# Linear attention and a Swish layer in one kernel: key-value products moved into the numerators' run, k's exponentials a block ahead of q's

## The chip, the cores and the metric

The kernel runs on one core of a Trainium2 chip. The metric is the device time of one execution in microseconds. Five runs of the kernel before gave a median of 286.03 us (285.89 to 286.53). One more execution was taken by the hardware profiler; all durations below are from that one.

## The reference

Linear attention for 8 batches of 8 heads, 576 positions and 64 channels, then a layer with a scaled Swish on the 4,608 rows of 512 that come out of it. All inputs and the output are float32.

```python
phi = lambda x: np.where(x > 0, x, np.exp(x) - 1.0) + 1.0
q_p, k_p = phi(q), phi(k)
kv  = einsum('bhsd,bhse->bhde', k_p, v);   z = sum(k_p, axis=2)
num = einsum('bhsd,bhde->bhse', q_p, kv)
den = einsum('bhsd,bhd->bhs', q_p, z)[..., None] + 1e-06
x = (num / den) as rows [4608, 512]
h = x @ w_in                              # w_in [512, 2048]
out = (h / (1 + exp(-beta * h))) @ w_out  # w_out [2048, 512]
```

## The kernel before

**Blocks.** One block of the second layer takes 512 rows: the first 512 positions of one batch, in four x tiles. The 64 positions left over of each batch make a ninth block. A block has two stages. In H (`h_phase`, L779) TensorE makes 16 tiles of h, four matmuls of 512 columns each (`h_mm`, L439), and ScalarE turns each into g with Silu (`silu`, L448). In Y (`y_phase`, L790) TensorE makes four tiles of the output, sixteen matmuls each (`y_mm`, L456), VectorE copies each out of PSUM and SyncE's queue writes it out (`y_out`, L469).

**Attention between the lines.** While block b runs, the attention of batch b+1 and b+2 is made in pieces that the program hangs between the matmuls. Two dictionaries, `sh` for H and `sy` for Y, say after which step of the stage a piece is issued (L811 to L834). H has 16 steps, one a tile; Y has 16 too, four a tile. Nothing reorders instructions: each engine works in the order in which they were issued, and tiles bring the waits. For block b, with n = b+1 and m = b+2, the kernel before does this:

- After step 8 of H, `kv_both(n)` (L230): 72 products of 64x64 (`k_quads`, L177) make kv and z of batch n in a PSUM tile of its own, and VectorE copies it to `kvd` (L239). In block 2, `odd_numers` (L335), the left-over numerators of batches 0 and 1, come just before.
- After the last step of H, `numers(n)` (L322): 72 products of 64x64 make the numerators and denominators of batch n, in two PSUM tiles of two banks (`nps`) and in two of the four buffers that H and Y tiles use too (`nps_m`). `norms` (L372) divides them on VectorE into x tiles.
- After steps 0 and 1 of Y, `x_trans_dma(n, t)` (L426): SyncE issues the transposes that bring the x tiles into `xT`, from which the next block's H reads.
- After step 3 of Y, phi of q of batch m (`phi_all`, L487): two exponentials on ScalarE (L144), then on VectorE max and min (L148, L155). phi(x) is min(exp(x), max(x, 0) + 1).
- After step 5 of Y, `q_trans_dma(m)` (L272): SyncE transposes phi of q by DMA. Then GpSimd issues the loads of q and k of batch m+1 (`load_kq`, L476); the q load is held until those transposes have landed (`hold`, L88), and the k load stands behind it in GpSimd's queue.
- After step 8 of Y, phi of k of batch m, and on GpSimd the two copies of v of batch m into `vaug` (`v_copy`, L171).
- After step 9 of Y, SyncE issues the load of v of batch m+1.

**Buffers.** There are three of q and k each (`xq`, `xk`, L51), two of v and `vaug`, four of the exponentials' result (`e`, L143), two of the large PSUM tiles (`num_tile`, L227) and four of the small ones (`mm_tile`, L453).

**Start.** Batch 0, the weights and batch 1 have a stage of their own (L556 to L770); the first block that follows the scheme is b = 1. In it, after step 2 of H, q, k and v of batch 3 are loaded. Two table loads a Y stage (`ACT_TABLE_LOAD`) switch ScalarE between exponential and Silu.

Of the kernel before, what the change touches and what calls it, by code (L numbers as in the profile page):

```python
# [9 lines left out]
BF16 = mybir.dt.bfloat16  # L10
# [6 lines left out]
def kernel(  # L17
# [10 lines left out]
    nc = tc.nc  # L28

    B, H, S, D = q.shape  # L30
    DM = H * D
    DFF = moe_w_in.shape[1]
    P = 128
    KC = DM // P
    FC = DFF // P
# [3 lines left out]
    EA = D + 1  # L39
# [8 lines left out]
    work = ctx.enter_context(tc.tile_pool(name="work", bufs=2))  # L48


    NX = 3  # L51
# [28 lines left out]
    def load(eng, dst, src, b, h0=0, n=4):  # L80

        rows = src[b].rearrange("h (g j) d -> (h g) (j d)", j=J)
        return eng.dma_start(  # L83
            out=dst[:, h0 : h0 + n].rearrange("p h j d -> p h (j d)"),
            in_=rows.rearrange("(i p) e -> p i e", p=P)[:, h0 : h0 + n],
        )

    def hold(d, after):  # L88
        tc.add_manual_dep(d.ins, after.ins.name, SYNC, reason="share of the queues")
# [48 lines left out]
    st = {}  # L138

    def phi_part(b, a, pr, x, j0=0, j1=J):  # L140

        if j0 == 0:
            st[b, a, pr, "e"] = work.tile([P, 2, J, D], BF16, tag="e", name="e", bufs=4)  # L143
        nc.scalar.activation(st[b, a, pr, "e"][:, :, j0:j1], x[:, :, j0:j1], ACTF.Exp)  # L144
# [6 lines left out]
    def phi_tile(b, a):  # L151
        st[b, a] = work.tile([P, 2, J, P], BF16, tag=f"phi{a}", name=f"phi_{a}")

    def phi_min(b, a, pr, j0=0, j1=J):
        nc.vector.tensor_tensor(  # L155
            st[b, a][:, pr, j0:j1].rearrange("p j (h d) -> p j h d", h=2),
            st[b, a, pr, "e"][:, :, j0:j1].rearrange("p h j d -> p j h d"),
            st[b, a, pr, "r"][:, :, j0:j1].rearrange("p h j d -> p j h d"),
            ALU.min,
        )  # L160
# [5 lines left out]
    def xin(b, a, pr):  # L166
        if b == 0 and a == "q":
            return q0f[:, places(b, pr)]
        return (xk if a == "k" else xq)[b % NX][:, places(b, pr)]

    def v_copy(eng, b, pr):  # L171
        src = vb[b % 2] if b == 2 else vf[b % 2]
        eng.tensor_copy(  # L173
            vaug[b % 2][:, pr, :, :, 0:D], src[:, places(b, pr)].rearrange("p h j d -> p j h d")
        )

    def k_quads(b, pr, dst, mov):  # L177

        for j in range(J):
            for h in range(2):  # L180
                for hh in range(2):
                    r = slice(hh * G, (hh + 1) * G)
                    c = slice(h * D, (h + 1) * D)
                    nc.tensor.matmul(  # L184
                        dst[hh][c], st[b, "k"][r, pr, j, c], mov(r, j, h),
                        start=(j == 0), stop=(j == J - 1), skip_group_check=True,
                    )
# [39 lines left out]
    def num_tile(name):  # L227
        return numps.tile([P, 2, 512], F32, tag="num", name=name)

    def kv_both(b):  # L230

        t = num_tile("kvp")
        for pr in range(2):
            k_quads(
                b, pr, [t[:, hh, pr * EA : (pr + 1) * EA] for hh in range(2)],
                lambda r, j, h: vaug[b % 2][r, pr, j, h, 0:EA],
            )
        st[b, "kvd"] = work.tile([P, 2, 2 * EA], BF16, tag="kv_bd", name="kvd")
        nc.vector.tensor_copy(st[b, "kvd"], t[:, :, 0 : 2 * EA])  # L239

# [31 lines left out]
    def q_trans_dma(b):  # L272
        st[b, "qTd"] = work.tile([P, 4 * J, G], BF16, tag="qT", name="qTd")
        for hh in range(2):
            st[b, "qTd", "dma"] = nc.sync.dma_start_transpose(
                out=st[b, "qTd"][:, hh * 2 * J : (hh + 1) * 2 * J],
                in_=st[b, "q"][hh * G : (hh + 1) * G].rearrange("p a j c -> p (a j c)"),
            )
# [40 lines left out]
                e = e0 + 2 * (pr - prs[0]) + hh  # L319
                quads(b, dst, e, lambda c, pr=pr: (pr, 2 * t + c), hh, pr)  # L320

    def numers(b):  # L322
        pairs = [num_tile("nps") for _ in range(2)]
        odd = [mm_tile("nps_m") for _ in range(2)]
        for k in range(2):
            dst = [pairs[k][:, h] for h in range(2)]
            numer_tile(b, dst, k)
            numer_tile(b, dst, 2, (k,), 4)
        numer_tile(b, odd, 3)
        for hh in range(2):  # L330
            quads(b, odd, 4 + hh, lambda c: (c, J - 1), hh, None)
        st[b, "nps"] = pairs, odd


    def odd_numers():  # L335
# [90 lines left out]
    def x_trans_dma(b, t):  # L426
        xv = st[b, "xs", t].rearrange("p n d -> p (n d)")
        if t < NT - 1:
            nc.sync.dma_start_transpose(out=x_dst(b, t), in_=xv)
            return  # L430

        for pr in range(2):
            nc.sync.dma_start_transpose(
                out=xT_tail[:, places(b, pr), b * G : (b + 1) * G],
                in_=xv[pr * G : (pr + 1) * G, 0 : 2 * P],
            )
# [16 lines left out]
    def mm_tile(name):  # L453
        return mmps.tile([P, 512], F32, tag="mm", name=name)

    def y_mm(b, t, i, yp, c0=0, c1=512):  # L456
        for c in range(4):
            ff = 4 * i + c
            nc.tensor.matmul(  # L459
                yp[:, c0:c1],  # L460
                g_sb[b % 2][:, ff, t * P : (t + 1) * P],
                w_out_sb[i][:, c, c0:c1],
                start=(ff == 0), stop=(ff == FC - 1), skip_group_check=True,
            )
# [8 lines left out]
            dst = rows(b, 2 * t + i) if b < B else rows(2 * t + i, J - 1)  # L473
            queues[i].dma_start(out=dst[:, c0:c1], in_=y_sb[i * G : (i + 1) * G, c0:c1])

    def load_kq(b, after=None):  # L476
        if b < B:
            d = load(nc.gpsimd, xq[b % NX], q, b)
            if after is not None:
                hold(d, after)  # L480
            load(nc.gpsimd, xk[b % NX], k, b)

    def load_v(b):
        if b < B:
            load(nc.sync, vf[b % 2], v, b)

    def phi_all(b, a):  # L487
        phi_tile(b, a)
        for pr in range(2):
            phi_part(b, a, pr, xin(b, a, pr))  # L490
        for pr in range(2):
            phi_relu(b, a, pr, xin(b, a, pr))
        for pr in range(2):
            phi_min(b, a, pr)


    beta_c = consts.tile([P, FC], F32)
# [277 lines left out]
    def run(side, n):  # L775
        for f in side.get(n, ()):
            f()

    def h_phase(b, x, side):  # L779
        for ff in range(FC):  # L780

            if b == 1 and ff in (3, 4):
                hp = num_tile("h_ps2")[:, 0]
            else:
                hp = mm_tile("h_ps")
            h_mm(b, x, ff, hp)
            silu(b, ff, hp)
            run(side, ff)

    def y_phase(b, side, last=False):  # L790
        for t in range(4):
            if last and t == 3:
                for c0, c1 in ((0, 320), (320, 512)):
                    yp = mm_tile("y_ps")
                    for i in range(4):
                        y_mm(b, t, i, yp, c0, c1)
                    y_out(b, t, yp, c0, c1, (nc.sync, nc.scalar))
                break
            yp = mm_tile("y_ps")
            for i in range(4):  # L800
                y_mm(b, t, i, yp)
                if i < 3:
                    run(side, 4 * t + i)
            y_out(b, t, yp)
            run(side, 4 * t + 3)

    def at(side, n, *fs):
        side.setdefault(n, []).extend(fs)


    for b in range(1, B + 1):  # L811
        n = b + 1
        sh, sy = {}, {}
        if b == 1:
            at(sh, 0, lambda: q_trans_dma(2))
            at(sh, 1, lambda: [v_copy(nc.gpsimd, 2, pr) for pr in range(2)])
            at(sh, 6, lambda: q_odd_trans(1, num_tile("qop")[:, 0].bitcast(BF16)[:, 0:256]))
            at(sh, 2, lambda: load_kq(3, st[2, "qTd", "dma"]), lambda: load_v(3))
        if b == 2:
            at(sh, 8, odd_numers, odd_norms)  # L820
            at(sh, 9, lambda: [x_trans_dma(i, 4) for i in range(2)])
        if n < B:
            at(sh, 8, lambda: kv_both(n))
            at(sh, FC - 1, lambda: numers(n), lambda: [norms(n, k) for k in range(3)])
            for t in range(NT):
                at(sy, t // 3, lambda t=t: x_trans_dma(n, t))
        if n + 1 < B:
            m = n + 1
            at(sy, 3, lambda: phi_all(m, "q"))
            at(sy, 5, lambda: q_trans_dma(m), lambda: load_kq(m + 1, st[m, "qTd", "dma"]))  # L830
            at(sy, 8, lambda: phi_all(m, "k"), lambda: [v_copy(nc.gpsimd, m, pr) for pr in range(2)])
            at(sy, 9, lambda: load_v(m + 1))
        h_phase(b, xT[b % 3] if b < B else xT_tail, sh)
        y_phase(b, sy, last=(b == B))  # L834

# [29 lines left out]
```

## Time and profile before

| What | Value |
|---|---|
| Median of five runs | 286.03 us (285.89 to 286.53) |
| The profiled execution's own time | 286.03 us |
| Its span, first to last instruction | 284.2 us |
| Mean granted TensorE clock | 0.998 |
| Busy: TensorE matmuls, ScalarE, VectorE, GpSimd | 98%, 56%, 37%, 13% of the span |
| Matmuls of Y (L459) | 127.2 us busy, x600 |
| Matmuls of H (L441) | 109.6 us busy, x496, and 14.0 us, x64, of the ninth block |
| kv products (L184, out of `vaug`) | 4.8 us busy, x432 |
| Numerators (L309) | 3.5 us busy, x288, and 2.4 us, x144 |
| Exponentials (L144) of k, of q | 1.15 us each |
| Loads of q, of k | 10.7 and 12.9 us from issue to landing (median) |

A line of the profile names the source line, the engine, the operation, what it writes and reads (`out<-in`) and how many there were. In a timeline the first two numbers are the start and the length in microseconds; what stands in brackets is the idle time of the engine before it and what ended it. PE is TensorE, ACT ScalarE, DVE VectorE, POOL GpSimd, SPq the queue of SyncE, which issues transfers. In the view of stretches the columns are the stretch, its length, busy time and number of instructions of each engine (PE, PEld, DVE, ACT, POOL), the granted clock, the share of the 16 DMA engines that is busy (over 1 where packets overlap) and GB/s. "DMA to landing" gives the least, the median and the longest time from an issue to its landing. A matmul's length in the trace is 379 ns, but the next starts 216 ns after it: they are pipelined, and start to start is what a matmul costs.

### The profile page before, as it was taken

How to read it: one execution, taken by the hardware profiler on the slowest of the kernel's cores; microseconds unless marked ns; L12 is line 12 of the kernel's file. 1: busy time of each engine (PE TensorE's matmuls, PEld its weight loads, DVE VectorE, ACT ScalarE, POOL GpSimd, SP SyncE). 2: the span in 40 equal slices, each digit the busy share in tenths (PEclk: the TensorE clock that was granted, in tenths of full speed). 3: DMA queues.
4: the chain of work that ended last, by engine and by line, in shares of the span. 5: the costliest groups of instructions: out<-in, count | busy, mean ns of one | idle time of the engine just before them, and what ended most of it. 6: DMA issues, size and time to landing. Idle time of an engine off the chain costs nothing.

```text
span 284.2 us, 5939 instructions
## 1 busy us (share of the span) xinstructions
PE 277.7 (98%) x2476; PEld 135.8 (48%) x2476; DVE 106.5 (37%) x256; ACT 160.3 (56%) x219; POOL 36.9 (13%) x51
## 2 busy tenths in 40 slices
PE   7999999999999999999999999999999999999994
PEld 2584457445444444444444444444444444444443
DVE  5832677708602670068005810492024100110012
ACT  5878587972866925793478437862750186028500
POOL 8732100310050003100310026000000000000000
PEclk9999999999999999999999999999999999999999
DMA  7999999669989349956896389637203510230032
GB/s 220 207 211 392 248 262 187 152 167 242 165 225 251 72 96 185 274 98 75 195 284 81 70 184 284 113 66 172 61 2 80 123 30 2 60 82 8 0 74 75
DMA packets 51723, 41.03 MB, mean 144 GB/s; under 512 B 31584, under 2 KB 43120, under 8 KB 51696
## 3 DMA queue, kind: packets, MB, share of 16 engines
q1 hardware_dynamic: 38800, 23.61, 34.9%
q0 software_dynamic: 12736, 16.91, 30.1%
q8 instruction: 19, 0.31, 0.5%
q10 hardware_dynamic: 160, 0.13, 0.2%
q14 instruction: 8, 0.07, 0.1%
HBM read 36.71 MB, written 9.44 MB: 162 GB/s over the span
## 4 chain that ended last, share of the span: by engine, by line
PE 81%; DMA 13%; POOL 2%; ACT 1%; issue 1%; DVE 0%; POOLq 0%; ACTq 0%
PE h_ps L441 39%; PE y_ps L459 39%; DMA xq<-in_q_dram 8%; DMA w_in<-in_moe_w_in_dram 5%; PE kvp L184 1%; PE nps L309 1%; POOL w_in L120 1%; ACT e L144 1%; POOL vf L83 1%; ACT xT L422 1%; PE nps_m L309 0%; POOL xk L83 0%; DVE y_sb L245 0%; POOL identity masks.py:199 0%; PE nps_o L343 0%
## 5 line engine op out<-in xcount | busy, mean ns | idle before, releaser
L449 ACT ACTIVATE g<-h_ps,beta_c 128x512 bf16<-128x512 f32 x144 | 97.8, 689 | 89.6 <-PE h_ps L441 89.1
L459 PE MATMUL y_ps<-w_out,g 128*128 128x512 bf16 (+3 forms) x600 | 127.2, 371 | 0.0
L441 PE MATMUL h_ps<-xT,w_in 128*128 128x512 bf16 x496 | 109.6, 379 | 0.4 <-ACT e L144 0.3
L459 PEld LDWEIGHTS <-g 128*128 128x128 bf16 x600 | 57.6, 98 | 64.0
L441 PEld LDWEIGHTS <-w_in 128*128 128x128 bf16 x560 | 54.1, 98 | 65.0 <-DVE y_sb L245 0.7
L245 DVE COPY y_sb<-y_ps 128x512 f32<-128x512 f32 (+2 forms) x37 | 24.8, 674 | 73.6 <-PE y_ps L459 72.4
L83 POOL DMA_DIRECT2D xq<-in_q_dram x7 | 5.2, 744 | 105.4 <-DMA qTd<-phi_q 86.3
L144 ACT ACTIVATE e<-xk 128x1152 bf16<-128x1152 bf16 x16 | 17.7, 1150 | 0.4 <-DMA xk<-in_k_dram 0.4
L144 ACT ACTIVATE e<-xq 128x1152 bf16<-128x1152 bf16 x14 | 15.6, 1155 | 1.4 <-DMA xq<-in_q_dram 1.4
L379 DVE TENSOR_SCALAR den<-nps 128x12 f32<-128x12 f32 x12 | 2.0, 165 | 35.6 <-PE nps L309 35.6
L239 DVE CAST kvd<-kvp 128x260 bf16<-128x260 f32 x6 | 2.6, 427 | 32.6 <-PE kvp L184 32.6
L441 PE MATMUL h_ps<-xT_tail,w_in 128*128 128x512 bf16 x64 | 14.0, 379 | 0.0
L155 DVE TENSOR_TENSOR phi_q<-e,r 128x1152 bf16<-128x1152 bf16 (+2 forms) x17 | 11.8, 722 | 4.7 <-ACT e L144 4.4
L370 DVE TENSOR_TENSOR xs<-nps,rden 128x512 bf16<-128x512 f32 (+1 forms) x24 | 12.3, 553 | 1.2 <-DMA xT_tail<-xs 0.8
L144 ACT ACT_TABLE_LOAD x6 | 7.7, 1283 | 8.5 <-DMA xq<-in_q_dram 8.4
L155 DVE TENSOR_TENSOR phi_k<-e,r 128x1152 bf16<-128x1152 bf16 x16 | 11.7, 764 | 0.0
L173 POOL CAST vaug<-vf 128x1152 bf16<-128x1152 f32 x10 | 11.2, 1159 | 1.9 <-DMA vf<-in_v_dram 1.9
L133 PE MATMUL warm_ps<-xT 128*128 128x512 bf16 x23 | 8.5, 519 | 1.5 <-DVE xT L96 1.5
L449 ACT ACT_TABLE_LOAD x6 | 7.7, 1283 | 0.1
L83 POOL DMA_DIRECT2D xk<-in_k_dram x9 | 6.8, 751 | 4.5 <-DMA g<-in_moe_w_out_dram 1.9
L706 DVE TENSOR_SCALAR w_out<-g,rbeta 128x512 bf16<-128x512 f32 x8 | 3.8, 537 | 8.9 <-DMA g<-in_moe_w_out_dram 8.9
L184 PEld LDWEIGHTS <-phi_k 64*64 64x64 bf16 x576 | 5.6, 106 | 3.3 <-issue 2.1
(96 smaller groups left out, 121.6 us busy)
## 6 DMA issues: line engine op xcount, KB each, us to landing
out_dram<-y_sb SPq DMA_DIRECT2D x70, 128.0 KB, 2.4
vf<-in_v_dram SPq DMA_DIRECT2D x5, 1152.0 KB, 6.6
xq<-in_q_dram POOLq DMA_DIRECT2D x7, 576.0 KB, 10.7
xk<-in_k_dram POOLq DMA_DIRECT2D x7, 576.0 KB, 12.9
w_in<-in_moe_w_in_dram POOLq DMA_DIRECT2D x4, 512.0 KB, 12.2
g<-in_moe_w_out_dram POOLq DMA_DIRECT2D x2, 1024.0 KB, 17.3
stage<-in_moe_w_out_dram POOLq DMA_DIRECT2D x2, 1024.0 KB, 20.9
stage<-in_q_dram SPq DMA_DIRECT2D x2, 576.0 KB, 4.1
```

The costliest lines, as they stand in the source:

```text
L83: return eng.dma_start(out=dst[:, h0 : h0 + n].rearrange("p h j d -> p h (j d)"), in_=rows.rearrange("(i p) e -> p i e", p=P)[:, h0 : h0 + n],
L133: nc.tensor.matmul(warm_ps[:, 0:cols], warm[:, 0:P], warm[:, 0:cols], start=True, stop=True)
L144: nc.scalar.activation(st[b, a, pr, "e"][:, :, j0:j1], x[:, :, j0:j1], ACTF.Exp)
L155: nc.vector.tensor_tensor(st[b, a][:, pr, j0:j1].rearrange("p j (h d) -> p j h d", h=2), st[b, a, pr, "e"][:, :, j0:j1].rearrange("p h j d ...
L173: eng.tensor_copy(vaug[b % 2][:, pr, :, :, 0:D], src[:, places(b, pr)].rearrange("p h j d -> p j h d"))
L184: nc.tensor.matmul(dst[hh][c], st[b, "k"][r, pr, j, c], mov(r, j, h), start=(j == 0), stop=(j == J - 1), skip_group_check=True,)
L245: eng.tensor_copy(dst, src)
L370: nc.vector.tensor_mul(out, num, rd[..., None].to_broadcast(list(num.shape)))
L441: nc.tensor.matmul(hp[:, c0:c1], w_in_sb[ff // 4][:, kc, (ff % 4) * P : (ff % 4 + 1) * P], x[:, kc, c0:c1], start=(kc == 0), stop=(kc == K ...
L449: nc.scalar.activation(g_sb[b % 2][:, ff, :], hp, ACTF.Silu, scale=beta_c[:, ff : ff + 1])
L459: nc.tensor.matmul(yp[:, c0:c1], g_sb[b % 2][:, ff, t * P : (t + 1) * P], w_out_sb[i][:, c, c0:c1], start=(ff == 0), stop=(ff == FC - 1), ...
L706: nc.vector.tensor_scalar(w_out_sb[i][:, c, :], w_out_f[i][:, c, :], rbeta[:, ff : ff + 1], None, ALU.mult,)
```

## The change

- `kv_both` stays for batches 2 and 3. From batch 4 on, the 72 kv products of batch m are issued at the head of `numers(n, m)`, in the last step of H, into columns of the `nps` tiles that the numerators leave free. Two copies after the normalising bring them to `kvd`, one for each pair of heads. `norms` is called inside `numers`.
- k's exponentials are issued a block before the rest of its phi: `phi_exps(m + 1, "k")` after step 10 of Y, `phi_rest(m, "k")` (max and min) after step 2 of the next H. The v copies of batch m move to step 6 of that H. k is loaded a block earlier: k of batch m+2 behind q of batch m+1. In block 1, k of batch 4 is loaded after q and k of batch 3, and phi of k of batch 3 stays in Y.
- In block 1, `numers(2)` moves from the end of H into Y, after step 1 of its first tile; the x transposes of batch 2 move to steps 2 and 3, so that the first output tile is issued before the fourth x tile's transpose. The last two tiles of this Y are made in two halves of 256 columns, each with its own sixteen matmuls; the pieces of their steps come in the second half.

```diff
+    def kv_pair(b, pr, dst):
+        k_quads(b, pr, dst, lambda r, j, h: vaug[b % 2][r, pr, j, h, 0:EA])
...
-    def numers(b):
+    def numers(b, after=None):
+
         pairs = [num_tile("nps") for _ in range(2)]
         odd = [mm_tile("nps_m") for _ in range(2)]
+        if after is not None:
+            for pr in range(2):
+                kv_pair(after, pr, [pairs[pr][:, hh, 6 * EA : 7 * EA] for hh in range(2)])
...
         st[b, "nps"] = pairs, odd
+        for k in range(3):
+            norms(b, k)
+        if after is not None:
+            st[after, "kvd"] = work.tile([P, 2, 2 * EA], BF16, tag="kv_bd", name="kvd")
+            for pr in range(2):
+                nc.vector.tensor_copy(
+                    st[after, "kvd"][:, :, pr * EA : (pr + 1) * EA],
+                    pairs[pr][:, :, 6 * EA : 7 * EA],
+                )
...
-            for i in range(4):
-                y_mm(b, t, i, yp)
-                if i < 3:
-                    run(side, 4 * t + i)
+            halves = ((0, 256), (256, 512)) if b == 1 and t > 1 else ((0, 512),)
+            for cols in halves:
+                for i in range(4):
+                    y_mm(b, t, i, yp, *cols)
+                    if i < 3 and cols is halves[-1]:
+                        run(side, 4 * t + i)
...
+        m = n + 1
         sh, sy = {}, {}
         if b == 1:
             at(sh, 0, lambda: q_trans_dma(2))
-            at(sh, 1, lambda: [v_copy(nc.gpsimd, 2, pr) for pr in range(2)])
+            at(sh, 1, lambda: v_copies(2))
+            at(sh, 2, lambda: load_q(3, st[2, "qTd", "dma"]), lambda: load_k(3))
+            at(sh, 2, lambda: load_v(3), lambda: load_k(4))
             at(sh, 6, lambda: q_odd_trans(1, num_tile("qop")[:, 0].bitcast(BF16)[:, 0:256]))
-            at(sh, 2, lambda: load_kq(3, st[2, "qTd", "dma"]), lambda: load_v(3))
-        if b == 2:
-            at(sh, 8, odd_numers, odd_norms)
-            at(sh, 9, lambda: [x_trans_dma(i, 4) for i in range(2)])
+            at(sh, 8, lambda: kv_both(2))
+            at(sy, 1, lambda: numers(2))
+        elif n < B:
+            if b == 2:
+                at(sh, 8, odd_numers, odd_norms, lambda: kv_both(3))
+                at(sh, 9, lambda: [x_trans_dma(i, 4) for i in range(2)])
+            if m < B:
+                at(sh, 2, lambda: phi_rest(m, "k"))
+                at(sh, 6, lambda: v_copies(m))
+            at(sh, FC - 1, lambda: numers(n, m if m < B else None))
         if n < B:
-            at(sh, 8, lambda: kv_both(n))
-            at(sh, FC - 1, lambda: numers(n), lambda: [norms(n, k) for k in range(3)])
             for t in range(NT):
-                at(sy, t // 3, lambda t=t: x_trans_dma(n, t))
-        if n + 1 < B:
-            m = n + 1
+                at(sy, t // 3 + (2 if b == 1 else 0), lambda t=t: x_trans_dma(n, t))
+        if m < B:
             at(sy, 3, lambda: phi_all(m, "q"))
-            at(sy, 5, lambda: q_trans_dma(m), lambda: load_kq(m + 1, st[m, "qTd", "dma"]))
-            at(sy, 8, lambda: phi_all(m, "k"), lambda: [v_copy(nc.gpsimd, m, pr) for pr in range(2)])
+            at(sy, 5, lambda: q_trans_dma(m), lambda: load_q(m + 1, st[m, "qTd", "dma"]))
+            at(sy, 5, lambda: load_k(m + 2))
+            if b == 1:
+                at(sy, 8, lambda: phi_all(3, "k"), lambda: v_copies(3))
             at(sy, 9, lambda: load_v(m + 1))
+            if m + 1 < B:
+                at(sy, 10, lambda: phi_exps(m + 1, "k"))
```

## The prediction

> **What bounds the kernel now.** I read the page first, then TensorE's own waits, then the chain that ended last, and then SyncE, GpSimd and the transfers around the one stage where the change moves transfers. All durations are of one profiled execution: span 284.2 us, its own time 286.03 us, so 1.8 us lie around the span. The median of the five runs is also 286.03 us, so a difference in the span is added to the median as it stands.
>
> ```profile
> PE 277.7 (98%) x2476; PEld 135.8 (48%) x2476; DVE 106.5 (37%) x256; ACT 160.3 (56%) x219; POOL 36.9 (13%) x51
> ```
>
> TensorE is busy for 98% of the span. Its waits (a view of its own) add up to 2.8 us, and the last of them ends at 49.07. From there to the last matmul it never waits: the time is the sum of what TensorE does. So a part of the change can pay only by giving TensorE less to do, and can cost by giving it more, or by making a first wait. The chain of waits shows where it does something other than stream (start, length, what):
>
> ```profile
> 86.43 0.25 PE nps_o L343 x16
> 86.68 0.64 PE kvp L184 x72
> ...
> 108.13 7.77 PE h_ps L441 x36
> 115.90 0.73 PE kvp L184 x72
> 116.63 6.15 PE h_ps L441 x28
> 122.78 0.51 PE nps L309 x48
> 123.29 0.23 PE nps_m L309 x24
> 123.51 13.92 PE y_ps L459 x64
> ```
>
> See two things. A run of 64x64 products costs more than its own length: the 28 matmuls after it take 6.15 where 36 undisturbed ones take 7.77 (28 of those: 6.04). And a run that follows another such run is cheaper (0.64 at 86.68) than one that follows full matmuls (0.73 at 115.90).
>
> **Part 1: kv of batches 4 to 7 joins the numerators of the batch ahead.** Nothing is removed but the border. Kv alone: from the end of the matmul before (115.90) to the end of the 28 after (122.78) are 6.88 us; less 28 x 0.2158 = 6.04 that leaves 0.84. Its 72 products start 8.3 ns apart in the trace, so 0.60 of it is work and 0.24 is border, in and out. Joined, one run meets the next after 22 ns instead of 8 (the step from nps_o to kvp at 86.5), so the price is about 0.61 and the saving 0.23. By the chain's coarser pieces it is 0.20 (0.73 - 0.64, and 6.15 - 6.04). Four blocks do it (batches 4, 5, 6, 7; 3 keeps its own place): 4 x 0.23 = **0.92 us less**, bounds 0.80 and 0.97.
>
> The cover: kv's result is not wanted until the next block's end, 28 us later. Its reading out becomes two copies behind the normalising, 0.28 to 0.43 each by the nearest rows (a 128x128 scale out of PSUM, the 128x260 copy now); VectorE sits idle 7.3 us before the odd normalising in such a stage. The numerators end 0.6 later in the stage's time, and with them the x transposes; in the second Y the fourth of these landed at 102.1 and its use is at 107.96.
>
> **Part 2: k's phi split.** The exponentials stay two of 1.15 us in Y, where ScalarE in the third block has 7.9 us idle; max and min (2 x 0.45 + 2 x 0.76 = 2.4 us) go to H, where VectorE idles. Nothing on the path. v's copies move from Y to H: v of batch 4 landed at 86.5, 1.7 later now (Part 4), copies 2.25, so 90.4; wanted at 93.4. Cost nothing; 3 us of cover.
>
> **Part 3: Y of block 1 in halves.** For its last two tiles 32 matmuls of 512 columns become 64 of 256.
>
> ```profile
> 45.15 0.60 PE L459 MATMUL y_ps<-w_out,g 128*128 128x256 bf16 x4
> 45.59 0.39 PE L417 MATMUL nps<-identity,xs 128*128 128x128 bf16 x4
> ```
>
> Four of 256 columns take 0.436 (next start less start), 0.109 each; a pair 0.218 against 0.2158. 32 x 0.0022 = **0.07 us more** (bounds 0 and 0.13, the latter by 0.11 each). The batch-2 numerators only change place: in and out of a run once, as before.
>
> **Part 4: the first Y stage, where transfers move.** Batch 2's numerators start at 65.66 instead of 63.94 (H's last matmul starts at 63.63; then eight of Y at 0.216 and 0.09 into the run), so everything behind them moves by 1.73: VectorE's normalising, and on SyncE's queue the transposes of x, one output tile now placed ahead of the fourth of them, the transposes of q, and the v load.
>
> ```profile
> 62.62 0.74 POOL L83 DMA_DIRECT2D xq<-in_q_dram  x1 [9.60 <-DMA qTd<-phi_q]
> 63.36 0.75 POOL L83 DMA_DIRECT2D xk<-in_k_dram  x1
> ...
> 81.20 0.74 POOL L83 DMA_DIRECT2D xq<-in_q_dram  x1 [17.10 <-ACT g L449]
> ```
> ```profile
> 65.56 5.77 SPq L429 DMA_TRANSPOSE xT<-xs  x4
> 71.43 2.69 SPq L433 DMA_TRANSPOSE xT_tail<-xs_odd  x2
> 74.22 1.18 SPq L474 DMA_DIRECT2D out_dram<-y_sb  x2
> 75.50 2.77 SPq L275 DMA_TRANSPOSE qTd<-phi_q  x2
> ```
> ```profile
> 66.00:70.00 4.00, 4.00 (x20) 1.82 (x19) 3.37 (x12) 0.00 (x0) 0.00 (x0) 1.00 1.21 206
> 72.00:74.50 2.50, 2.50 (x13) 1.18 (x12) 1.69 (x3) 2.50 (x3) 0.00 (x0) 1.00 1.27 185
> ```
> ```profile
> DMA to landing us min/median/max: 5.1/6.5/7.9
> ```
>
> The first two are GpSimd's and SyncE's issues, the third the DMA share of two stretches (next to last column: full), the fourth the landing of the x transposes in this stage. Elsewhere these land 2.3 us after issue; here 5.1 to 7.9, because q and k of batch 3 were issued before them: no transpose packet moves before 69.5, and the bulk only when k is nearly through (72.8). The change puts a third load, k of batch 4, right behind k of batch 3.
>
> The H stage of block 2 needs all four transposes at 78.50 + 0.07 = 78.57. The fourth landed at 75.16, 3.4 us early. What is put ahead of it: the load, 512 packets at some 183 per us, 2.8 us (3.3 by the two loads' landings, 69.96 and 73.25; 0 if the transposes were served first), and the output tile, 128 packets of 142 ns on 16 engines, 1.1. That gives 79.1 (79.6). Against it, 540 of the transposes' packets slipped in before the loads were done, and this trickle has three microseconds more to run: up to 0.8 off, 78.3. I take 78.8, that is a first wait of **0.2 us**; both ends stay (0 and 1.0; with the 1.73 us of later issue on top, 2.8).
>
> The Trainium skill ("DMA: Bandwidth & Descriptors", Queues, rings and completion order) says that a DMA engine takes turns between its queue rows packet by packet. By it the transposes would share from the start, the wait would be 0 and the time 285.2. The stretch from 65.6 to 69.5 above, without one transpose packet, speaks against it.
>
> Second use of the same shift: batch 3's v copies stand behind the q load, which waits for the transposes of q. They ended at 84.92 and kv of batch 3 started at 86.51. With 1.73 more they end at 86.65, and the half of kv that needs the second copy starts at 86.9. Hidden by 0.25, one for one beyond that.
>
> Third: ScalarE gets a third pair of exponentials here.
>
> ```profile
> 70.03 1.28 ACT L144 ACT_TABLE_LOAD   x1 [5.30 <-DMA xq<-in_q_dram]
> 73.45 2.20 ACT L144 ACTIVATE e<-xk 128x1152 bf16<-128x1152 bf16 x2
> ```
>
> k of batch 4 should land at 76.1 to 76.6; 2.2 of exponentials and 1.28 of table: 80.1. The first Silu may start as late as 81.3 (four buffers of H: 78.57 + 4 x 0.863 - 0.69). Hidden by 1.2.
>
> Fourth, a block later: the normalising of batch 3 waits for transposes behind the next loads (0.8 us now, until 96.48); 1.7 later it frees a Y buffer at 100.6 (98.9 now), wanted at 101.7 (101.05 now, 0.6 of kv and 0.07). Hidden by 1.
>
> **Sum.** 286.03 - 0.92 + 0.07 + 0.2 = 285.38, about **285.4 us**.
>
> **Rivals.**
> 1. *The fourth x transpose of batch 2 lands noticeably late.* For it: the full DMA share, the 79.1 to 79.6 above. Against: the trickle. A wait of 0.3 to 1.4 us gives 285.5 to 286.6, middle 285.9. The v copies can add to it only what they are later than H itself.
> 2. *The same transpose lands so late that the saving is lost: slower.* Place: first matmul of H in block 2. Price: the longer load (3.3), the output tile (1.1) and most of the 1.73 of later issue, which add if SyncE's issuing and the queue delay each other: 80.8 to 81.3, a wait of 2.2 to 2.8, about 287.5. It decides from a landing at 80.0 on. For it: all of SyncE's queue is back to back from 65.56 to 78. Against: the issue shift should drown in the wait for the loads.
> 3. *The joining saves nothing*, because products with another stationary operand and another output drain like a border: 286.03 + 0.07 + 0.2 = 286.3, at most. Against: the 22 ns at 86.5, which is just such a change.
>
> **How the numbers follow.** The measurement can tell about 0.2% (0.57 us) from no change; the borders are 285.46 and 286.60. Forecast 0.50; rival 1 0.27; rival 2 0.18; rival 3 0.05. Faster by over 0.2%: 0.50, the forecast. Within: rivals 1 and 3, 0.32. Slower: 0.18. Range: low 284.9 (saving 0.97, no wait, no price of the halves, and 0.16 for the runs' spread); high 287.0, which leaves out the far part of rival 2, about 0.1. The likeliest case alone holds 284.9 to 285.5.
>
> **What would show it.** Right: in blocks 2 to 5 one run of 144 products in 1.3 us, and the matmuls of H 64 in a row; TensorE's waits with at most 0.3 us on xT. Rival 1 or 2: a wait of L454's matmuls at about 78.6 for xT, with a landing over 79. Rival 3: pauses of 0.1 between kv and numerators. I am wrong if a wait turns up for another reason, above all on vaug at 86.9 or on ScalarE after 78.

## The result and the profile after

The changed kernel takes 286.83 us (median of 45 runs, 285.98 to 291.36) against 286.15 (87 runs) of the kernel before on the same chips: ratio 1.002, interval 1.0011 to 1.0029. It is slower by 0.2% where 0.2% less (285.4 us) was forecast. The time lies in the predicted range, above the forecast by 1.4 us. The profiled execution's own time is 286.9 us, its span 285.1 (before: 286.03 and 284.2); the granted clock is 1.00 throughout.

The first line is from the page (busy time, share of the span, instructions); the others are TensorE's waits: what waited for what, the sum in us, how often, the longest.

```profile
PE 276.6 (97%) x2508; PEld 138.9 (49%) x2508; DVE 106.0 (37%) x260; ACT 160.5 (56%) x219; POOL 37.1 (13%) x51
```
```profile
PE h_ps L454 <- issue: 0.8, 1, 0.8
PE tp L265 <- DVE phi_q L155: 0.8, 1, 0.8
...
PE kvp L184 <- POOL vaug L173: 0.2, 1, 0.2
```

TensorE is busy 1.1 us less than before, as the joining promised, and the span is 0.9 us longer: what was saved went into waits. Two of these lines lie where the change moves something and have no counterpart in the kernel before: L454, the matmuls of H, and `kvp` on `vaug`. (The `tp` line belongs to the first stage, ahead of everything the change touches; it is up to 1.6 us in the executions profiled here.) The timeline of TensorE in block 2 shows where they lie:

```profile
79.81 7.93 PE L454 MATMUL h_ps<-xT,w_in 128*128 128x512 bf16 x36 [0.85 <-issue]
87.67 0.32 PE L356 MATMUL nps_o<-kv,q_odd 64*64 64x65 bf16 x16
87.82 0.48 PE L184 MATMUL kvp<-vaug,phi_k 64*64 64x65 bf16 x36
88.56 0.48 PE L184 MATMUL kvp<-vaug,phi_k 64*64 64x65 bf16 x36 [0.25 <-POOL vaug L173]
88.97 6.22 PE L454 MATMUL h_ps<-xT,w_in 128*128 128x512 bf16 x28
95.11 0.80 PE L184 MATMUL nps<-vaug,phi_k 64*64 64x65 bf16 x72
95.73 0.61 PE L309 MATMUL nps<-kvd,qTd 64*64 64x65 bf16 x48
```

The first line is the first H matmul of block 2. The profile names no releaser for its wait ("issue"), but the fourth x transpose of batch 2 landed at 79.72, 0.09 before it. The third and fourth lines are kv of batch 3: in the kernel before it is one line of 72 products, here it breaks in two, and the second half waits for the second v copy. The last two lines are the new joined run: no pause between kv (72) and numerators (48).

The chain of waits of the same stretch (start, length, what) puts the two together:

```profile
79.05 5.19 DMA qTd<-phi_q
...
84.78 0.09 POOL xq L83
...
85.51 0.76 POOL xk L83
86.27 2.25 POOL vaug L173 x2
...
88.56 0.48 PE kvp L184 x36
89.03 6.15 PE h_ps L454 x28
95.18 0.73 PE nps L184 x72
95.92 0.42 PE nps L309 x48
96.34 0.23 PE nps_m L309 x24
96.57 13.92 PE y_ps L472 x64
110.49 13.81 PE h_ps L454 x64
```

Two things to see. H of block 2 is not on the chain at 79.8: the chain passes below it, from the transposes of q to the q load held for them, the k load, the v copies and kv of batch 3. A lateness at H is made up in a wait that would come anyway. And further down, H of block 3 is one piece of 64 matmuls in 13.81 us, where the kernel before had 7.77, 0.73 and 6.15.

Start of the last matmul, 280.35 before and 281.25 after, by stages: +0.22 ahead of block 1, not the change's; +0.08 the halves of Y in block 1; +1.01 from the end of the last Y matmul of block 1 to the first H matmul of block 2; +0.40 kv of batch 3 (1.02 instead of 0.60 long); -0.80 from there to the end. The sum is +0.91; +0.90 was measured.

### The profile page after: what moved, and what is told of

Same layout as the page of the kernel before. It is cut to its first block, busy times and chain, and to the rows that moved or that the text cites. A ratio compares the mean times of both kernels' runs of the same rounds, so it can differ in the third digit from the quotient of the medians.

```text
span 285.1 us, 6007 instructions
## 1 busy us (share of the span) xinstructions
PE 276.6 (97%) x2508; PEld 138.9 (49%) x2508; DVE 106.0 (37%) x260; ACT 160.5 (56%) x219; POOL 37.1 (13%) x51
## 4 chain that ended last, share of the span: by engine, by line
PE 78%; DMA 15%; POOL 3%; ACT 1%; issue 1%; DVE 0%; POOLq 0%; SPq 0%; ACTq 0%
PE y_ps L472 39%; PE h_ps L454 36%; DMA xq<-in_q_dram 8%; DMA w_in<-in_moe_w_in_dram 5%; DMA qTd<-phi_q 2%; PE nps L184 1%; POOL w_in L120 1%; PE nps L309 1%; ACT e L144 1%; POOL vaug L173 1%; POOL xk L83 1%; POOL vf L83 1%; ACT xT L435 1%; PE nps_m L309 0%; PE kvp L184 0%
## 5 line engine op out<-in xcount | busy, mean ns | idle before, releaser
L454 PE MATMUL h_ps<-xT,w_in 128*128 128x512 bf16 x496 | 108.9, 379 | 1.2 <-issue 0.8
L472 PEld LDWEIGHTS <-g 128*128 128x128 bf16 x632 | 60.8, 98 | 61.1
L454 PEld LDWEIGHTS <-w_in 128*128 128x128 bf16 x560 | 54.4, 98 | 66.6 <-issue 1.3
L454 PE MATMUL h_ps<-xT_tail,w_in 128*128 128x512 bf16 x64 | 14.0, 379 | 0.0
L133 PE MATMUL warm_ps<-xT 128*128 128x512 bf16 x23 | 7.7, 477 | 1.5 <-DVE xT L96 1.5
L148 DVE TENSOR_SCALAR r<-xk 128x1152 bf16<-128x1152 bf16 x16 | 6.7, 454 | 0.0
```

What stands on the lines that cost most here:

```text
L133: nc.tensor.matmul(warm_ps[:, 0:cols], warm[:, 0:P], warm[:, 0:cols], start=True, stop=True)
L148: nc.vector.tensor_scalar(r, x, 0.0, 1.0, ALU.max, ALU.add)
L454: nc.tensor.matmul(hp[:, c0:c1], w_in_sb[ff // 4][:, kc, (ff % 4) * P : (ff % 4 + 1) * P], x[:, kc, c0:c1], start=(kc == 0), stop=(kc == K ...
L472: nc.tensor.matmul(yp[:, c0:c1], g_sb[b % 2][:, ff, t * P : (t + 1) * P], w_out_sb[i][:, c, c0:c1], start=(ff == 0), stop=(ff == FC - 1), ...
```

## The experiments

My theory after this: the two waits of block 2, 1.4 us, take what the joining saves. They have two causes that both delay the same queues: the k load of batch 4 issued ahead of the x transposes, and the numerators of batch 2 issued 1.7 us later. Rivals: the joining saves less than it seems; the first stage's spread makes the difference; the halves cost more than their 0.08 us. Unless it is said otherwise, an edit is to the changed kernel, and ratios are to the kernel before, run on the same chip.

### Numerators of batch 2 back at the end of H

```diff
-            at(sy, 1, lambda: numers(2))
+            at(sh, FC - 1, lambda: numers(2))
...
-                at(sy, t // 3 + (2 if b == 1 else 0), lambda t=t: x_trans_dma(n, t))
+                at(sy, t // 3, lambda t=t: x_trans_dma(n, t))
```

> Changed kernel with batch 2's numerators back at the end of H of block 1 and the x transposes back at steps 0 and 1 of Y; the third load and the halves stay. Theory (the third load, k of batch 4, holds up the transposes of x and, through them, those of q): the x transposes are issued 1.7 us earlier but still wait for the loads; the fourth lands at 78.2 to 78.8 instead of 79.7, so H of block 2 starts up to 0.9 us earlier; but the q transposes still wait for the first x transpose (77 to 77.5), so the v copies of batch 3 end at about 88 and kv of batch 3 waits 1 us or more. In all 286.4 to 286.8 (0.0 to 0.4 less than the change). Rival (the later issue of the numerators alone makes both waits, the third load does not matter): both waits go, about 285.5.

Measured: 286.16 us (285.4 to 287.58), ratio 0.9997 [0.9983, 1.001], 0.7 less than the change: less than the theory's 286.4 to 286.8 and more than the rival's 285.5. In its profiled execution (285.46, span 283.7, one of the fastest) neither wait is there: the fourth x transpose landed at 78.13, and the v copies ended at 87.04, as they were wanted. A wait of kv that I had expected is missing in this execution; the executions spread over 2 us, and the kernel with both repairs below shows that others have it.

### Without the early load of k of batch 4

```diff
+        if (b, a) == (4, "k"):
+            return xk[0][:, places(b, pr)]
...
-            at(sh, 2, lambda: load_v(3), lambda: load_k(4))
+            at(sh, 2, lambda: load_v(3))
```

This kernel leaves out one load; phi of k of batch 4 is made from other data in the same shape.

> Changed kernel without the early load of k of batch 4; the phi of k of batch 4 is made from batch 3's k instead, so the products of batch 4 are not the reference's and one load of 576 KB is left out. All else stays. Theory (the third load): the fourth x transpose lands at about 76.5, H of block 2 starts without a wait, the q transposes land at about 83 and kv of batch 3 waits 0 to 0.3 us; 285.5 to 285.8 (about 1.0 to 1.3 less than the change). Rival (the later issue of the numerators): both waits stay, 286.7.

Measured: 286.04 (285.48 to 286.52), 0.9998 [0.999, 1.0007], 0.8 less than the change, a little more than the 285.5 to 285.8 expected. In the profile (285.48) the four x transposes landed 3.7 to 7.7 us after issue, the fourth at 76.98, and H doesn't wait; kv of batch 3 still takes 1.05 instead of 0.81 (the view's lengths of the 72). Either cause alone keeps part of the loss.

### v copies of batch 3 ahead of the held q load

```diff
             at(sy, 3, lambda: phi_all(m, "q"))
+            if b == 1:
+                at(sy, 4, lambda: v_copies(3))
...
-                at(sy, 8, lambda: phi_all(3, "k"), lambda: v_copies(3))
+                at(sy, 8, lambda: phi_all(3, "k"))
```

> Changed kernel with the two v copies of batch 3 issued on GpSimd after step 4 of Y in block 1, ahead of the held q load, instead of after step 8 behind it. Theory (the wait of kv of batch 3 is only its place in GpSimd's queue): kv of batch 3 does not wait, H of block 2 still starts 0.9 us late; 0.3 to 0.5 less than the change, 286.3 to 286.5. Rival (v itself, or phi of k, is late): no difference, 286.8.

Measured: 285.64 (285.23 to 286.68), 0.9985 [0.9976, 0.9994]. One move on GpSimd's queue takes 1.2 us off the change, more than either cause above. In the profiled execution (285.56) the v copies start at 66.02, when v lands, instead of 86.24:

```profile
66.02 2.24 POOL L173 CAST vaug<-vf 128x1152 bf16<-128x1152 f32 x2 [1.22 <-DMA vf<-in_v_dram]
```

The fourth x transpose landed at 78.61; H starts 0.19 late, and kv takes 0.73 instead of 0.60, without a wait that the profile lists. The chain above says why 1.2 and not the 0.4 of the second wait: GpSimd's chain alone was late by the sum of both, so the wait of H hid behind it, and it is not the same in all executions.

### Both repairs, and the load left out with the v copies early

The first of these two kernels takes the edits of the first and third experiment together (numerators back, v copies early, halves kept); the second those of the second and third.

> Changed kernel with batch 2's numerators back at the end of H of block 1 (x transposes at steps 0 and 1) and the v copies of batch 3 ahead of the held q load. Theory (the waits of block 1 and 2 are these two places and nothing else): both waits go in nearly every execution, the four joined runs save 0.75 us, the halves cost 0.07: 285.3 to 285.6, below both kernels. Rival (the executions differ for another reason, such as the fetch of instructions): 286.0 to 286.3, as with the numerators alone put back.

> Changed kernel without the early load of k of batch 4 (its phi is made from batch 3's k, so batch 4's products are not the reference's and one load of 576 KB is left out) and with the v copies of batch 3 ahead of the held q load. Theory (without the third load what varied was the wait for the v copies): neither wait is left, 285.2 to 285.5. Rival (the third load matters little once the v copies are out of the way): the same as with the v copies alone, 285.6.

Measured: 285.40 (285.22 to 285.99), 0.9971 [0.9958, 0.9984] for the first, and 285.32 (285.18 to 285.45), 0.9965 [0.9952, 0.9979] for the second. In both the waits of block 2 are gone. The first computes all that the reference wants and beats both kernels: 0.75 us less than before, which is what the change's ledger gives without its waits (-0.80 and +0.08). So the joining does save what the ledger says, and the rival falls; so does the one that put the difference down to the first stage, which is the same program here. The first kernel differs from the one with the numerators back by the early v copies alone, and takes 0.76 us less: the wait of kv that the profile there did not show is in other executions. From v copies early it differs by the numerators' place alone: 0.24 less, so with GpSimd's chain out of the way little is left of the wait of H. The repaired kernel's waits of TensorE, all of them in the start and none on `xT` or `vaug`:

```profile
PE warm_ps L133 <- DVE xT L96: 1.5, 1, 1.5
PE nps L194 <- DVE phi_k L155: 0.8, 2, 0.5
PE tp L265 <- DVE phi_q L155: 0.3, 1, 0.3
PE h_ps L454 <- ACT e L144: 0.3, 1, 0.3
PE nps L184 <- PE zt L194: 0.2, 1, 0.2
```

### One more load behind k of batch 4

The load of q of batch 4 is there twice, here and in its own place.

```diff
-            at(sh, 2, lambda: load_v(3), lambda: load_k(4))
+            at(sh, 2, lambda: load_v(3), lambda: load_k(4), lambda: load(nc.gpsimd, xq[1], q, 4))
```

> Changed kernel with one more load of 576 KB behind the load of k of batch 4 in H of block 1 (q of batch 4 into its buffer, loaded again at its own place later; nothing waits for the first). Theory (the x transposes stand behind the loads that were issued before them): the fourth x transpose lands 3 us later, at about 82, and H of block 2 starts 2.5 to 3 us later than in the change: 289 to 290. Rival (the transposes share the DMA engines with the loads, turn by turn): less than 1 us more, under 287.9.

Measured: 289.48 (288.78 to 290.16), 1.011 [1.0085, 1.0134], 2.65 more than the change. Of the four executions the two with a mean granted clock of 1.00 took 288.78 and 288.89, the two with 0.992 and 0.993 290.16 and 290.06, so part of the 2.65 is a slower clock. TensorE's timeline in block 2 (start, length, idle time before and its releaser), and how long the x transposes took to land:

```profile
82.05 7.93 PE L454 MATMUL h_ps<-xT,w_in 128*128 128x512 bf16 x36 [2.62 <-DMA xT<-xs]
```
```profile
DMA to landing us min/median/max: 7.7/9.0/10.9
```

The added load landed at 80.35; of the x transposes, all issued by 74.29, three landed at 80.28, 80.65 and 81.96. This settles what is ahead of what: the transposes land when the loads issued before them are through, at most the first of them with the load before the last. The other executions (the last load here is the last q or k load issued ahead of the x transposes; times in us):

| Kernel | Last load landed | First x transpose landed | Fourth landed | Held q load issued | Second v copy ended |
|---|---|---|---|---|---|
| before | 73.25 | 73.42 | 75.16 | 81.20 | 84.92 |
| before, with halves (below) | 73.57 | 73.74 | 75.50 | 82.15 | 85.87 |
| change | 77.59 | 77.51 | 79.72 | 84.78 | 88.50 |
| numerators back | 76.49 | 74.39 | 78.13 | 83.33 | 87.04 |
| no k load | 74.74 | 74.93 | 76.98 | 83.36 | 87.08 |
| v copies early | 76.61 | 76.62 | 78.61 | 84.23 | 68.26 |
| no halves (below) | 75.77 | 75.98 | 77.90 | 83.47 | 87.20 |
| no halves, padded (below) | 76.67 | 76.50 | 78.43 | 84.11 | 87.84 |
| both repairs | 77.09 | 74.56 | 78.55 | 84.11 | 68.38 |
| both repairs, no halves (below) | 77.36 | 74.48 | 78.80 | 83.40 | 68.74 |
| no k load, v copies early | 72.65 | 73.25 | 75.98 | 84.16 | 68.67 |
| no loads, no halves (below) | 76.64 | 76.64 | 78.72 | left out | 68.47 |

The fourth lands 1.4 to 2.2 us after the last load, but for one row: with no k load and the v copies early the load was through before the fourth was issued (73.49), and it landed 2.5 us after that. Five rows (the change, v copies early, no halves, padded, no loads) issue the same transfers in the same order up to there, and the fourth landed at 77.9 to 79.7: it varies by 1.8 us between executions. The held q load varies too, by 1.0 us in the two kernels with neither cause (81.20 and 82.15).

### Without the halves of Y

```diff
-            halves = ((0, 256), (256, 512)) if b == 1 and t > 1 else ((0, 512),)
+            halves = ((0, 512),)
```

> Changed kernel with the last two Y tiles of block 1 whole again (512 columns). Theory: TensorE reaches H of block 2 0.08 us earlier and waits 0.08 us longer for the fourth x transpose, which lands at the same time; 286.7 to 286.9, no difference to the change. Rival (the halves themselves cost): 0.3 us or more less than the change.

Measured: 290.28 (288.38 to 292.45), 1.0143 [1.0106, 1.018]. Leaving out 0.08 us of work makes the kernel 3.5 us slower; everything I expected missed by that. TensorE's timeline in the last H step of block 2, where the joined run stands:

```profile
93.81 0.81 PE L184 MATMUL nps<-vaug,phi_k 64*64 64x65 bf16 x72
94.43 0.61 PE L309 MATMUL nps<-kvd,qTd 64*64 64x65 bf16 x48
94.86 0.34 PE L309 MATMUL nps_m<-kvd,qTd 64*64 64x65 bf16 x16
97.67 0.26 PE L309 MATMUL nps_m<-kvd,qTd 64*64 64x65 bf16 x8 [2.47 <-issue]
```

16 of a group's 24 products run, then nothing for 2.5 us, then the last 8. They read and write the same tiles as the 16 before, so no tile can have been missing. Soon after, the clock drops: in the view of stretches (stretch, length, busy time and count of PE, PEld, DVE, ACT, POOL, then granted clock, DMA share, GB/s) what starts at 99 runs at half speed, the next stretch at full. The third line is the first stretch in a kernel below that pauses too, but keeps its clock.

```profile
99.00:102.50 3.50, 3.50 (x10) 1.26 (x9) 1.05 (x5) 2.52 (x3) 0.00 (x0) 0.51 0.74 54
104.00:108.00 4.00, 4.00 (x21) 1.79 (x19) 2.67 (x5) 0.00 (x0) 0.00 (x0) 1.00 0.39 89
...
99.00:102.50 3.50, 3.50 (x18) 1.59 (x17) 2.03 (x8) 2.51 (x3) 0.00 (x0) 1.00 0.69 53
```

10 matmuls stand where that kernel has 18, eight fewer at 0.216 us each: 1.7 us lost in this stretch.

What does TensorE wait for, if no tile? The page has a transfer queue that no line of the kernel issues:

```profile
q8 instruction: 19, 0.31, 0.4%
```

19 packets of 16,384 bytes: by the name, the instructions themselves. Each takes 0.9 to 2.1 us. In the trace one of these packets starts at 95.40 in this kernel, just after the pause began (95.20), and ends at 96.35; TensorE goes on at 97.67, and the trace does not show what fills the 1.3 us between. Until then the loads of q of batch 4 and k of batch 5 keep the DMA engines full (a share of 1.24 from 92.5 to 95.0, 0.52 from 95 to 98). In the changed kernel the nearest packets start at 92.30 and 96.88, the first ahead of its joined run. The suspicion: the halves change nothing in the work, but move where the next block of instructions is needed. With them, 32 matmuls more, each with its weight load, stand ahead of the joined run: 64 instructions; the joined run is 288 instructions in 1.27 us. Three kernels test it.

### 64 instructions of padding in place of the halves

```diff
-            halves = ((0, 256), (256, 512)) if b == 1 and t > 1 else ((0, 512),)
+            halves = ((0, 512),)
...
+        if b == 2:
+            for n in range(32):
+                c, h = n // 2 % 2, n % 2
+                r = slice(h * D, (h + 1) * D)
+                nc.tensor.matmul(
+                    pairs[1][c * G : (c + 1) * G, h, 500 + n // 4 : 501 + n // 4],
+                    st[b, "qTd"][r, c, :], st[b, "kvd"][r, 0, 0:1],
+                    start=True, stop=True, skip_group_check=True,
+                )
```

The 32 products of one column write places that nobody reads.

> The kernel without halves (290.3 us) with 32 products of one column added behind batch 2's numerators in block 1: as many TensorE instructions as the halves add (64), and no other effect of the halves. Theory (in the kernel without halves TensorE runs out of instructions: the fetch of the next 16 KB comes 2 us late, behind the loads, just as 288 instructions of kv and numerators pass in 1.3 us; the halves only shift where the fetch falls): the 2.5 us pause in the run of block 2 and the slow clock behind it go, at a price of 0.3 us for the products: 286.5 to 287.3. Rival (the halves help by their length or by their columns): the pause stays, 290 to 290.6.

Measured: 287.05 (286.03 to 289.06), 1.0033 [1.0012, 1.0054]: 3.2 us less than without halves, and about the change's time. The same place:

```profile
94.45 0.81 PE L184 MATMUL nps<-vaug,phi_k 64*64 64x65 bf16 x72
95.07 0.61 PE L309 MATMUL nps<-kvd,qTd 64*64 64x65 bf16 x48
95.50 0.41 PE L309 MATMUL nps_m<-kvd,qTd 64*64 64x65 bf16 x24
```

All 24 products in one go, and an instruction packet at 91.74. It is the number of instructions that the halves bring, not the halves. Nor is it the time at which the run comes: it starts at 93.57 in the kernel with both repairs, at 93.81 in the kernel without halves, at 94.45 here and at 95.11 in the change, and only the one without halves pauses.

### Without halves and without the loads in the way

```diff
+        if (b, a) == (4, "q"):
+            return xq[0][:, places(b, pr)]
+        if (b, a) == (5, "k"):
+            return xk[1][:, places(b, pr)]
...
-        if b < B:
+        if b < B and b != 4:
             hold(load(nc.gpsimd, xq[b % NX], q, b), after)
...
-        if b < B:
+        if b < B and b != 5:
             load(nc.gpsimd, xk[b % NX], k, b)
...
-            halves = ((0, 256), (256, 512)) if b == 1 and t > 1 else ((0, 512),)
+            halves = ((0, 512),)
```

It leaves out the loads of q of batch 4 and k of batch 5 and uses other batches' data in their place.

> The kernel without halves (290.3 us) without the loads of q of batch 4 and k of batch 5 (their phi is made from q of batch 3 and k of batch 4, so the products of these batches are not the reference's and two loads of 576 KB are left out), which in that kernel run from 86 to 97 us. Theory (the fetch waits on its DMA engine behind these loads): the fetch before the joined run of block 2 lands in time, the pause is gone or under 0.5 us; 285.5 to 286.5. Rival (256 instructions in 1.2 us are too many for any fetch): the pause stays, at least 1 us, 287.5 or more.

Measured: 286.22 (285.53 to 288.37), 1.0009 [0.9981, 1.0036]. No pause in the joined run, with TensorE's instructions those of the kernel that paused; the instruction packet starts at 92.40 instead of 95.40.

```profile
93.72 0.81 PE L188 MATMUL nps<-vaug,phi_k 64*64 64x65 bf16 x72
94.33 0.72 PE L313 MATMUL nps<-kvd,qTd 64*64 64x65 bf16 x48
94.87 0.41 PE L313 MATMUL nps_m<-kvd,qTd 64*64 64x65 bf16 x24
```

The packets keep step with TensorE's instructions, not with the time. Counted up to the start of this packet (the view of stretches; the counts of PE and PEld are matmuls and weight loads), in this kernel, without halves and in the change:

```profile
0.00:92.40 92.40, 88.37 (x963) 47.22 (x976) 49.78 (x120) 67.19 (x99) 25.20 (x38) 1.00 0.98 221
0.00:95.40 95.40, 91.12 (x1104) 48.98 (x1116) 50.20 (x123) 69.82 (x102) 26.65 (x40) 1.00 1.02 226
0.00:92.30 92.30, 87.40 (x1000) 49.47 (x1001) 49.79 (x120) 66.15 (x97) 26.62 (x40) 1.00 1.04 226
```

That is 1,939 instructions here and 2,001 in the change, which has 64 more ahead of this place. It is also 2,001 padded and with the extra load, where the packet comes at 91.74 and 94.31. Without halves it is 2,220: the packet comes 281 instructions, or 3.0 us, after its place.

Three of its ten executions took about 288 us. Their mean granted clock was 0.993 and 0.994, that of the others 0.997 to 1.000, so a stretch at half clock is likely in them; none of the three was profiled.

### The repaired kernel without halves, and the kernel before with them

The first takes the edit of the halves to the kernel with both repairs; the second adds the halves, and nothing else, to the kernel before.

> The kernel with the numerators put back and the v copies ahead (285.4 us), with the last two Y tiles of block 1 whole again: 64 TensorE instructions fewer, no wait left in blocks 1 and 2. Theory (where the fetch of instructions falls decides, apart from the transfers of block 1): the pause of 2 to 2.7 us in the joined run of block 2 is back, with the slow clock behind it in some executions; 287.5 to 290. Rival (the pause came from the waits of block 1 and 2, which shifted the run against the loads): no pause, 285.3.

> The kernel before with the halves of the last two Y tiles of block 1, nothing else. Theory (the halves cost their 0.07 us, and where no run is longer than 144 instructions a shift of the fetch by 64 does nothing): 0.0 to 0.2 us more than before, 286.1 to 286.3. Rival (the halves gain something of their own): 285.8 or less.

Measured: 289.54 (287.86 to 292.77), 1.0101 [1.007, 1.0133] for the first: without the waits of block 2 the pause is the same, at the same place, with an instruction packet at 95.41, again at 2,220 instructions.

```profile
PE nps_m L309 <- issue: 2.5, 1, 2.5
```

In its profiled execution (288.25) the clock stayed at 1.00, so the pause alone is 2.5 us, and the half clock is a second price that not every execution pays: of the two kernels that pause, the executions with a mean clock of 1.00 took 287.9 to 288.5 us, those with 0.994 or less 289.5 and more. The second kernel took 286.17 (285.82 to 287.61), 1.0001 [0.9983, 1.0019]: where kv and numerators stand apart, 144 instructions each, the halves are worth nothing.

## Why the prediction was wrong, step by step

- **What bounds the kernel**: right. All of the time is what TensorE does, plus its waits; the ledger closes by them.
- **Part 1, the joining**: right, a little too large: 0.80 for four blocks instead of 0.92. The joined numerators ran at 9.1 ns a product instead of 8.6 (and 25 ns for the change of operand, where 22 were taken), so each run saves 0.20. That is the figure of the chain's coarser pieces, which I had named as the lower bound.
- **Part 2, phi of k in two parts**: right, no wait. The v copies of batch 4 ended at 91.88, wanted at 95.11.
- **Part 3, the halves**: the price was right, 0.08 against 0.07. What was not seen is that 64 instructions more or fewer decide over 3 to 4 us in this kernel; that the halves are a price and nothing else was right for the kernel before only.
- **Part 4, the first wait**: the place was right, the size was not in this execution: 1.0 instead of 0.2. The landing was put at 78.8 and measured at 79.72; in four other executions with the same order of transfers it was 77.9 to 78.7. By the medians the size was about right: v copies early still has this wait (0.19 in its profile) and takes 0.24 more than both repairs, though their intervals overlap. The two k loads landed 4.2 us apart (73.41 and 77.59), not 2.8 to 3.3. The trickle of transposes ran ahead of the load as expected, but it brought no transpose home early: 1,084 of their packets, as many as two transposes have (512 each), had moved by 77.0, and the first whole transpose landed at 77.51, with the load. (The 540 packets of the prediction are a count up to 72.0; up to that load's landing at 73.25 there are 1,046.) The view of the DMA queues in the change shows two phases, 67.5 to 71 and 72.5 to 75 (q0 carries GpSimd's loads, q1 SyncE's transfers; packets, MB, share of 16 engines):

```profile
q0 software_dynamic: 638, 0.72, 119.7%
...
q0 software_dynamic: 320, 0.37, 88.0%
q1 hardware_dynamic: 337, 0.09, 30.7%
```

The rule of the Trainium skill that I weighed there ("DMA: Bandwidth & Descriptors", Queues, rings and completion order: turns between queue rows, packet by packet) agrees with the second phase, about one packet for one. In the first, from the first issue at 67.51, no transpose packet moved until 71.29; in undisturbed stages the first one moves 1.2 us after the issue.
- **Part 4, "Second use of the same shift ... Hidden by 0.25, one for one beyond that": the step that failed.** It moved the held q load by the 1.73 us of later issue alone, to 82.93, and the v copies to 86.65. Measured: 84.78 and 88.50. The transposes of q stand behind those of x on SyncE's queue; what I had charged to the x transposes for the load ahead of them I did not charge to those of q:

```profile
77.72 3.02 SPq L275 DMA_TRANSPOSE qTd<-phi_q  x2
```
```profile
DMA to landing us min/median/max: 3.5/3.6/3.8
...
DMA to landing us min/median/max: 3.8/4.5/5.2
```

These are their issues in the change (75.50 before) and their landings before and in the change. The second was issued 2.15 us later than before (79.05 instead of 76.90), where 1.73 was counted, and landed 5.2 us after its issue instead of 3.75, where nothing was counted. Against 81.20 before, the held load is 2.1 to 2.9 us later with the k load alone (numerators back and both repairs, with and without halves), 2.2 and 3.0 with the later numerators alone (the two kernels without that load), and 2.3 to 3.6 with both: the causes do not add up, and the executions vary as much as they differ. Of both, less the 1.73 that were counted and 0.25 of cover, 0.3 to 1.6 remains late; the profiles show 0.27 (without halves), 0.61 (padded) and 1.41 (the change, H's wait with it). The early v copies, which touch this chain alone, gave back 1.2 us.
- **Part 4, third and fourth**: right, no wait. k of batch 4 landed at 77.59, a microsecond later than estimated, and ScalarE's first Silu began at 81.20, 0.1 ahead of the 81.3 that were allowed; H began late as well, and nobody waited for it.
- **Rivals**: the first named the place and, with "0.3 to 1.4 us", the sum of the waits. It priced the v copies as an addition to H's wait; it is the other way round, their chain is the longer one. The second rival's landing of 80.0 was not reached; the kernel is slower all the same, by the v copies. The third is refuted by the repaired kernel. That the measured time lies in the range owes to the room left for the first rival: the term that failed stood at nothing.

What stays open: the changed kernel's executions spread from 286 to 288 us and more, and only one of them was profiled; how the two waits share the rest is told only by the differences between kernels. That the pause is a late fetch of TensorE's instructions is argued from the packet's place in TensorE's count, from the padding that ends it and from the left-out loads that end it; the request for the packet is not in the trace. Why the packet is held up behind the loads in two kernels, and passes the same loads in time in those with 64 instructions more, is not shown.

## What to carry to other kernels

When a transfer is put ahead of others in a queue, charge it to every transfer behind it and follow each to its last reader; here the second reader cost more than the first. An engine that only issues and copies (here GpSimd) can carry the chain: look at what is queued behind a held load, and put ahead of it what has its data already. A kernel that gets much slower when a little work is taken out should be looked at for pauses in the middle of a group of equal instructions, with no tile missing.

## What the hardware showed that I had not expected

- SyncE's transposes land when GpSimd's loads issued before them are through, up to 10.9 us after their issue; one more load of 576 KB moved three of the four by 2.2 to 2.4 us.
- TensorE stopped for 2.5 us inside a group of like products, in two kernels, in a joined run whose 288 instructions take 1.3 us undisturbed, with loads filling the DMA engines. The Trainium skill ("Runtime: NRT & Kernel Launch", Instruction fetch mechanics) says that instructions come in blocks of 16 KiB, 256 at a time, by a DMA queue, and that the cost of crossing a block is "mostly hidden". The 16,384-byte packets agree; if the pause is such a crossing, as argued above, its 2.5 us were not hidden.
- After the pause the granted clock was 0.51 over 3.5 us in one execution, at a price of 1.7 us, and 1.00 in the other.
